# A retention layer with a token-mixing layer: tables and masks moved between engines, one pair form exchanged for another, the order planned anew

## The chip, the cores and the metric

The kernel runs on one core of a Trainium2 chip. The core has five engines that run side by side, each with its own instruction stream in a fixed order: TensorE (PE, matrix products), VectorE (DVE), ScalarE (ACT), GpSimd (POOL) and SyncE (SP, which here only issues transfers). Waits between them are semaphores set in when the program is built. SBUF is the working memory of 128 partitions; PSUM has eight banks of 128 x 512 float32, which PE writes and DVE and ACT read. The metric is the time of one execution in device microseconds. The kernel before was timed three times: 152.68, 157.84 and 153.59 us, median 153.59.

## The reference

Inputs q, k and v are float32 of shape (4, 8, 768, 64): batch, heads, tokens, width. Each head has a decay gamma = 1 - 2^(-5-h).

```
state = gamma * state + k[t] (outer) v[t]
y[t]  = (q[t] @ state) / 8
x     = y with the heads side by side           # (4, 768, 512)
W     = (x @ w_q) (x @ w_k)^T / 8               # tokens x tokens
out   = relu(W @ x) @ w_out                     # (4, 768, 512)
```

## The kernel before, in words

**Pairs.** The 768 tokens of a batch are three pairs of two chunks of 128 tokens, so there are twelve pairs over four batches (pair p is pair p % 3 of batch p // 3). Within a chunk the recurrence is computed as masked scores times v; between chunks a 64 x 64 state per head is carried in PSUM bank 7. The decay is applied as factors: v is multiplied by gamma^-t when it is cast to bfloat16, and the result by gamma^t.

**Kinds.** The string KINDS gives each pair a form. Form "2" (two tokens to a partition) keeps k and v as they are loaded, with two neighbouring tokens in one partition; its scores (L523), states, and products (L620, L631, L650) are made of more and smaller matmuls. Form "R" loads in the same way, but the casts (ck, cv) copy each 64-partition half into a one-token layout, four instructions instead of two, and then uses fewer matmuls (L537, L610, L664). Form "M" is R for k; its v is loaded already in the one-token layout, by four transfers of 256-byte rows (L177), and cast by two instructions of 128 partitions (L373) with the factor table fvM. Before, KINDS is 2R2RRR2RRMMM.

**Steps.** For each pair: loads Lk, Lq, Lv into one of 27 slots of the tile `stage`; casts ck, cq, cv; transposes trk, trq on PE into PSUM and their copies ek, eq (tiles kT, qT); scores sc by halves, and eat (L555), which multiplies them by the mask; st adds to the state and es copies it; in and ia form the product with the state and with the masked scores; ex (L685) multiplies by the factors fy into x; xt and exT transpose x. The mixing layer follows: wqk with its copy ew (tile m), zm per batch with its copy ez, mx and relu r (L798, L800), pj (L805) with w_out, eo copies the result to a slot, and S stores it.

**Order.** ORDER is a list of steps written out by a planner; the loop at the end of the kernel emits them one by one. A token such as `sc.7.0@05` is a step, its pair, its half and its PSUM banks; `:A`, `:V` and `:P` give the engine (ACT, DVE, POOL); `=4` gives a slot; `fill` is a matmul on a zero tile. Each engine executes its steps in this order. The framework adds a wait wherever a step touches what an earlier step of another engine still uses, slots, buffers and banks included. A step on two banks takes them as one strided slice:

```python
def two32(b):
    b0, b1 = b[:2]
    return banks[:, b0 : b1 + 1 : b1 - b0]
```

**Tables and masks.** The function `mask` makes a mask on POOL by a memset and an affine_select, twice where the partitions 64 to 127 have another offset, and copies the half over (L272 to L283). It is called by the tokens consts.2 and consts.R of ORDER, which stand among the first casts. The token constv.M, at about a third of ORDER, makes the table fvM: two iotas, a copy and a product on POOL (L230, L304, L305), then an Exp on ACT (L306). The tables fv and fy are made ahead of ORDER by DVE and ACT (L242 to L261).

The transfers are issued in the order of the L tokens on SP's queue, but for the first load, whose two halves go out on the queues of ACT and SP (FIRST).

Of the kernel before, what the change touches and what calls it, by code (L numbers as in the profile page):

```python
# [32 lines left out]
ck.7.1:P trq.5@45a xt.3@45b st.4.1 r.2.0:A r.2.1:A in.4.1@23 in.4.0@23 mx.0@01 exT.3:V cq.7.0:P  # L33
eq.5:A r.0.0:A ek.5:V ia.4.1@23 ia.4.0@23 wqk.3@4 r.0.1:A es.4.1:A sc.5.1@56 sc.5.0@01 cv.7.0:P
cv.7.1:P cv.8.1:P ex.4:V cv.8.0:P st.5.0 eat.5.0:V WO.0:A xt.4@2 pj.2.1@3 eat.5.1:V eo.2.1:A=12
pj.2.0@0 cv.9.0:P es.5.0:A ia.5.0@13 exT.4:V in.5.0@13 in.5.1@13 mx.1@56 r.1.0:V ia.5.1@13 ex.5:V
ew.3:V eo.2.0:A=12 pj.0.0@0 pj.0.1@2 ck.8.0:A xt.5@13a exT.5:V r.1.1:A eo.0.0:A=13 cq.6.1:A
trk.8@13b trk.6@04a trq.6@04b wqk.4@5 eq.6:A cq.8.0:A ek.8:V ek.6:V wqk.5@6 st.6.0 sc.6.0@04
cq.8.1:A ew.5:A ew.4:V sc.6.1@15 ck.10.1:P zm.1.0@3 ck.7.0:A eo.0.1:V=13 zm.1.1@3 cv.9.1:P eat.6.0:V
eat.6.1:V ez.1:A cq.7.1:A pj.1.1@6 cq.10.0:P cq.10.1:P cq.11.0:P cq.11.1:P trk.7@04a trq.8@04b  # L40
ck.11.0:P ck.11.1:P ek.7:V eo.1.1:A=15 mx.3@23 trq.7@15a pj.1.0@6 r.3.1:A r.3.0:A es.6.0:A eq.8:V
eq.7:V sc.8.1@04 cv.10.1:P cv.10.0:P mx.5@23 st.6.1 eo.1.0:A=15 r.5.1:A cq.9.1:A eat.8.1:V cq.9.0:A
r.5.0:A es.6.1:A ia.6.1@16 ia.6.0@16 in.6.1@16 ex.6:V sc.7.0@05 pj.3.1@4 st.7.0 sc.8.0@16 sc.7.1@23
eat.7.0:V eo.3.1:A=16 es.7.0:A pj.5.1@4 ck.9.0:A ck.9.1:A in.7.0@05 in.7.1@05 st.7.1 eat.7.1:V
ia.7.1@05 eat.8.0:V ia.7.0@05 trq.9@2 pj.3.0@3 ex.7:V xt.6@16a trk.9@16b eo.5.1:A=17 eq.9:A es.7.1:A
mx.4@05 r.4.0:A eo.3.0:V=16 st.8.0 r.4.1:A pj.5.0@2 ia.8.0@34 S.3 es.8.0:A ek.9:V exT.6:V
eo.5.0:A=17 sc.9.0@05 cv.11.0:P in.8.1@34 in.8.0@34 sc.9.1@16 st.9.0 S.5 es.9.0:A ck.10.0:A
eat.9.0:V ia.8.1@34 cv.11.1:P wqk.6@2 xt.7@0 pj.4.0@5 ew.6:A ex.8:V eat.9.1:V trk.10@2 st.9.1
trq.10@34a xt.8@34b in.9.1@16 eo.4.0:V=14 exT.7:A ek.10:A eq.10:V ia.9.0@16 ia.9.1@16 ex.9:V
pj.4.1@2 sc.10.1@05 exT.8:A eo.4.1:A=14 trq.11@34b sc.10.0@16 trk.11@34a wqk.8@2 eat.10.1:V ek.11:V  # L50
es.9.1:A eq.11:A S.0 ew.8:A wqk.7@0 eat.10.0:V ew.7:A sc.11.0@34 sc.11.1@25 st.10.0 zm.2.0@0
zm.2.1@0 es.10.0:A eat.11.1:V ez.2:A eat.11.0:V st.10.1 xt.9@1 es.10.1:A exT.9:A ia.10.1@25
ia.10.0@25 st.11.0 mx.6@06 es.11.0:A r.6.0:V r.6.1:A in.10.1@25 in.10.0@25 wqk.9@1 ia.11.0@34
ia.11.1@34 mx.7@06 in.11.1@34 in.11.0@34 ex.10:V pj.6.0@2 pj.6.1@5 r.7.0:A r.7.1:V ex.11:V mx.8@06
xt.10@34a xt.11@34b eo.6.0:A=19 eo.6.1:A=19 ew.9:V exT.11:V pj.7.1@1 wqk.11@5 exT.10:A wqk.10@3
r.8.1:A ew.10:A pj.8.1@4 ew.11:A r.8.0:A eo.7.1:V=20 zm.3.0@3 eo.8.1:V=18 zm.3.1@3 pj.7.0@0 ez.3:A
# [18 lines left out]
def kernel(  # L75
# [17 lines left out]

    nc = tc.nc
# [6 lines left out]
    U = 2  # L101
# [58 lines left out]
    def load(name, p, slot, part=None, eng=None):  # L160
# [7 lines left out]
        if KINDS[p] == "N" and name != "q":  # L168
# [60 lines left out]
    def iota(t, pattern, base, step, dtype=FP32):  # L229
# [5 lines left out]
    row = const_pool.tile([128, 3], mybir.dt.int32, name="row")  # L235
    tok = const_pool.tile([128, 1], FP32, name="tok")
# [5 lines left out]
    nc.vector.tensor_scalar(  # L242
        out=row[:, 1:2], in0=row[:, 0:1], scalar1=1, scalar2=U * (TG - 1), op0=ALU.logical_shift_left,
        op1=ALU.bitwise_and,
    )
    nc.vector.tensor_single_scalar(row[:, 2:3], row[:, 0:1], 6, op=ALU.logical_shift_right)
    nc.vector.tensor_tensor(out=tok, in0=row[:, 1:2], in1=row[:, 2:3], op=ALU.add)
# [5 lines left out]
    fy = const_pool.tile([128, NP * 2, H], FP32, name="fy")  # L253
    nc.vector.scalar_tensor_tensor(out=ty, in0=ty, scalar=tok, in1=ln_h, op0=ALU.add, op1=ALU.mult)
    nc.scalar.activation(out=fy, in_=ty, func=ACT.Exp)
# [6 lines left out]

    identity = const_pool.tile([128, 128], BF16, name="identity")
    make_identity(nc, identity)

    def mask(name, nj, step, base2):
        t = const_pool.tile([128, nj, U, TG], BF16, name=name)
        parts = [(t, 0)]
        if base2 is not None:
            parts.append((const_pool.tile([128, nj, U, TG], BF16, name=name + "_b"), base2))  # L270
        for a, base in parts:
            nc.gpsimd.memset(a, 1.0)  # L272
            nc.gpsimd.affine_select(
                out=a,
                in_=a,
                compare_op=ALU.is_ge,
                fill=0.0,
                base=base,
                pattern=[[-1, nj], [1, U], [U, TG]],
                channel_multiplier=-step,  # L280
            )
        if base2 is not None:
            nc.gpsimd.tensor_copy(out=t[64:128], in_=parts[1][0][64:128])  # L283
        return t.rearrange("p j u t -> p j (u t)")

    masks = {}
    fvs = {}

    def consts(kind):
        if kind == "2":  # L290
            masks["2"] = mask("mask2", 2, 2, 128)
        elif kind == "N":
            masks["N"] = mask("maskN", 1, 1, None)
        else:
            masks["R"] = mask("maskR", 1, 2, 127)

    def consts_v(kind):
        t = const_pool.tile([128, NP * 2, H], FP32, name="tv" + kind)
        f = const_pool.tile([128, NP * 2, H], FP32, name="fv" + kind)
        iota(t, [[C, NP * 2], [0, H]], 0, 1 if kind == "N" else 2)  # L300
        if kind == "M":
            t2 = const_pool.tile([128, NP * 2, H], FP32, name="tv2" + kind)
            iota(t2, [[C, NP * 2], [0, H]], 1 - C, 2)
            nc.gpsimd.tensor_copy(out=t[64:128], in_=t2[64:128])  # L304
        nc.gpsimd.tensor_tensor(out=t, in0=t, in1=ln_n, op=ALU.mult)  # L305
        nc.scalar.activation(out=f, in_=t, func=ACT.Exp)  # L306
        fvs[kind] = f
# [81 lines left out]
    def cq(e, b, p, x):  # L389
        st = pairs[p]  # L390
        if "qs" not in st:
# [491 lines left out]
```

## Time and profile before

| | |
|---|---|
| runs | 152.68, 157.84, 153.59 us; median 153.59 |
| profiled execution | 154.91 us, of which the span is 153.2 |
| mean granted TensorE clock | 0.833 |
| PE busy / DVE / ACT / POOL | 102.7 / 72.9 / 65.4 / 60.6 us |
| read from and written to memory | 20.19 and 6.29 MB |

The span goes from the first to the last instruction of the profiled execution. In the timelines a row is: start, duration, engine, line, operation, output and input, count, and in brackets the idle time of that engine before it with what ended it. The loads fill about the first 70 us; the stores come in the last third. The granted clock is a share of TensorE's full speed.

### The profile page before, as it was taken

To read this page: it belongs to the slowest core of one execution; us is meant where nothing else is said; L and a number is where in the kernel's file an instruction comes from. 1 tells how busy PE (TensorE), PEld (TensorE's weight loads), DVE (VectorE), ACT (ScalarE), POOL (GpSimd) and SP (SyncE) were. 2 spreads that over 40 slices of the span, in tenths; PEclk is the share of its full clock that TensorE was granted. 3 is DMA by queue.
4 is the path that set the end of the run, shared out by engine and by line. 5 is a ranking of instruction groups with operands and counts; after the bars stand their busy time and mean duration, and the time that the engine had idled before them with its cause. 6 is when DMAs were issued, how large, how long until landed. Compare 5 with 4: busy or idle time off the path is not lost.

```text
span 153.2 us, 3907 instructions
## 1 busy us (share of the span) xinstructions
PE 102.7 (67%) x1667; PEld 70.4 (46%) x1684; DVE 72.9 (48%) x117; ACT 65.4 (43%) x116; POOL 60.6 (40%) x89
## 2 busy tenths in 40 slices
PE   6958875599720997865365674569573766495990
PEld 2345554588520763743342443257452655263440
DVE  4045994567760376483533413143725733433460
ACT  4154256619404737537510705244244160435541
POOL 7599779879396699999100000000000000000000
PEclk9986999659985589999857655556999699999999
DMA  3999999999999999984000000342000000076394
GB/s 96 346 347 347 343 279 287 336 315 288 273 282 300 322 296 283 287 187 95 4 0 0 4 0 0 137 166 112 0 4 0 0 0 4 0 295 255 147 351 191
DMA packets 47169, 26.73 MB, mean 174 GB/s; under 512 B 8240, under 2 KB 44080, under 8 KB 47152
## 3 DMA queue, kind: packets, MB, share of 16 engines
q1 hardware_dynamic: 46624, 26.22, 56.1%
q10 hardware_dynamic: 528, 0.26, 0.6%
q8 instruction: 13, 0.21, 0.5%
q14 instruction: 4, 0.03, 0.1%
HBM read 20.19 MB, written 6.29 MB: 173 GB/s over the span
## 4 chain that ended last, share of the span: by engine, by line
PE 37%; SPq 21%; DVE 17%; ACT 9%; DMA 5%; issue 5%; POOL 4%; DVEq 0%; ACTq 0%; POOLq 0%
SPq L182 17%; PE banks L805 12%; DVE at L555 6%; DMA stage<-in_k_dram 5%; DVE x L685 5%; ACT relu L798 5%; PE banks L537 3%; SPq L199 3%; PE banks L664 3%; PE banks L727 2%; PE banks L738 2%; ACT qT L145 2%; PE banks L764 2%; DVE kT L146 2%; PE banks L694 2%
## 5 line engine op out<-in xcount | busy, mean ns | idle before, releaser
L805 PE MATMUL banks<-wout_sb,relu 128*128 128x512 bf16 x84 | 23.9, 406 | 9.5 <-DVE x L685 3.5
L555 DVE TENSOR_TENSOR at<-banks,maskR 128x1024 bf16<-128x1024 f32 x18 | 21.6, 1220 | 18.0 <-PE banks L537 7.6
L382 POOL TENSOR_TENSOR vs<-stage,fv 64x512 bf16<-64x512 f32 x24 | 25.0, 1043 | 2.9 <-DMA stage<-in_v_dram 1.5
L685 DVE TENSOR_TENSOR x<-banks,fy 128x1024 bf16<-128x1024 f32 x12 | 14.7, 1221 | 17.8 <-PE banks L664 7.7
L145 ACT COPY stage<-banks 128x512 f32<-128x512 f32 x15 | 8.7, 588 | 23.5 <-DVE at L555 6.9
L805 PEld LDWEIGHTS <-relu 128*128 128x128 bf16 x96 | 9.1, 103 | 18.4 <-issue 10.5
L145 ACT CAST ks<-stage 64x512 bf16<-64x512 f32 (+1 forms) x23 | 14.1, 616 | 6.6 <-DMA stage<-in_k_dram 6.3
L798 ACT ACTIVATE relu<-banks 128x512 bf16<-128x512 f32 x19 | 10.8, 597 | 11.8 <-PE banks L805 6.2
L146 POOL CAST ks<-stage 64x512 bf16<-64x512 f32 (+1 forms) x18 | 11.0, 609 | 5.7 <-DMA stage<-in_k_dram 5.0
L537 PE MATMUL banks<-qT,kT 64*128 64x128 bf16 x144 | 9.0, 263 | 5.7 <-DVE at L555 2.3
L328 PE MATMUL banks<-warm 128*128 128x512 bf16 x23 | 9.6, 575 | 1.8 <-DVE warm L218 1.3
L146 DVE COPY stage<-banks 128x512 f32<-128x512 f32 x9 | 6.1, 688 | 9.5 <-ACT relu L798 7.0
L537 PEld LDWEIGHTS <-kT 64*128 64x128 bf16 x144 | 6.0, 115 | 7.9 <-issue 6.6
L610 PE MATMUL banks<-s,qT 64*128 64x64 bf16 x128 | 4.2, 206 | 8.0 <-ACT relu L798 7.7
L664 PE MATMUL banks<-vs,at 128*128 128x64 bf16 x144 | 7.8, 209 | 2.6 <-DVE at L555 2.5
L727 PE MATMUL banks<-xT,wqk_w 128*128 128x256 bf16 x48 | 8.6, 309 | 1.4 <-DVE at L555 1.4
L145 ACT CAST qs<-stage 128x512 bf16<-128x512 f32 x13 | 7.7, 619 | 3.8 <-DMA stage<-in_q_dram 3.8
L555 DVE TENSOR_TENSOR at<-banks,mask 128x1024 bf16<-128x1024 f32 x6 | 7.2, 1222 | 3.6 <-ACT wqk_w L145 1.6
L571 PE MATMUL banks<-vs,ks 128*64 128x64 bf16 (+1 forms) x200 | 8.0, 217 | 1.3 <-POOL vs L363 0.9
L738 PE MATMUL banks<-wqk_w,xT 128*128 128x64 bf16 x96 | 8.7, 268 | 0.0
L664 PEld LDWEIGHTS <-at 128*128 128x128 bf16 x144 | 6.5, 108 | 4.5 <-issue 3.5
L146 DVE COPY kT<-banks 128x1024 bf16<-128x1024 bf16 x8 | 5.4, 685 | 5.9 <-PE banks L664 3.1
(89 smaller groups left out, 165.5 us busy)
## 6 DMA issues: line engine op xcount, KB each, us to landing
stage<-in_k_dram SPq DMA_DIRECT2D x12, 512.0 KB, 6.4
stage<-in_q_dram SPq DMA_DIRECT2D x11, 512.0 KB, 7.0
stage<-in_v_dram SPq DMA_DIRECT2D x9, 512.0 KB, 6.9
out_dram<-stage SPq DMA_DIRECT2D x9, 512.0 KB, 2.9
stage<-in_v_dram SPq DMA_DIRECT2D x12, 128.0 KB, 3.8
out_dram<-stage SPq DMA_DIRECT2D x6, 256.0 KB, 2.0
stage<-in_moe_w_out_dram SPq DMA_DIRECT2D x4, 256.0 KB, 4.5
stage<-in_q_dram ACTq DMA_DIRECT2D x1, 256.0 KB, 4.1
```

The lines of the kernel that those rows point to most:

```text
L145: return nc.scalar.copy(out=out, in_=in_)
L146: return ENGINES[e].tensor_copy(out=out, in_=in_)
L182: eng.dma_start(out=st.rearrange("g (h f) -> g h f", h=H)[:, hs], in_=src.rearrange("h (g j) d -> g h (j d)", j=2)[:, hs],)
L382: eng.tensor_tensor(out=st["vs"][rows(j), c].rearrange("p hp x d -> p (hp x) d"), in0=src[rows(c), :, j], in1=fv[rows(c), cp, :, j].to_bro ...
L537: nc.tensor.matmul(out=at[:, x, hi, c], lhsT=kT[rows(x), hp, c], rhs=qT[rows(x), c, hp], start=(hi == 0 and c == 0), stop=(hi == 1 and c = ...
L555: ENGINES[e].tensor_tensor(out=st["at", half].rearrange("p x hi j t -> p x (hi j t)").rearrange("p x (n f) -> p x n f", n=n), in0=st["at_p ...
L664: nc.tensor.matmul(out=y[:, x, c, hp, :], lhsT=at[:, x, hi, c, :], rhs=vr[:, c, hp, x, :], start=first(p, x), stop=False, skip_group_check ...
L685: ENGINES[e].tensor_tensor(out=dst, in0=src, in1=f.to_broadcast([128, 2, H, D]), op=ALU.mult)
L727: nc.tensor.matmul(out=ps[:, 128:384], lhsT=wqk_sb[:, a, 0 : 2 * DH], rhs=st["xT"][:, a].rearrange("p c t -> p (c t)"), start=(a == 0), st ...
L738: nc.tensor.matmul(out=wk[:, c], lhsT=st["xT"][:, a, c, :], rhs=wqk_sb[:, a, 2 * DH :], start=False, stop=(a == NDM - 1), skip_group_check ...
L798: nc.scalar.activation(out=st["relu", c], in_=src, func=ACT.Relu)
L805: nc.tensor.matmul(out=bank32(b[0]), lhsT=st["relu", c][:, a // 2, a % 2, :], rhs=wout_sb[:, a, :], start=(a == 0), stop=(a == NDM - 1),)
```

## The change

Tables: the argument of the Exp for the M pairs (now fvm) is formed by DVE from a per-partition token number, and its Exp stands in ACT's prologue beside the other two. Masks: an iota `tf` holds the token number of each column, and DVE compares it with the token number of the partition, once per mask plane. The tokens consts and constv are gone. KINDS becomes RR2RRRRRMMMM: pairs 0 and 6 go from form 2 to R, pair 8 from R to M, and pair 2 alone keeps form 2. FIRST is now k of pair 0. ORDER is a new list: other engines for some steps, other banks, other places for the fills (35 matmuls instead of 28) and the loads. Code for a layout with U = 8 is added and not used, since U is 2; trq is written in a more general way and does the same.

```diff
-KINDS = "2R2RRR2RRMMM"
-FIRST = ('q', 0, 0)
+KINDS = "RR2RRRRRMMMM"
+FIRST = ('k', 0, 0)
...
-    nc.vector.scalar_tensor_tensor(out=ty, in0=ty, scalar=tok, in1=ln_h, op0=ALU.add, op1=ALU.mult)
-    nc.scalar.activation(out=fy, in_=ty, func=ACT.Exp)
+    def decay(name, tok, ln):
+        t = const_pool.tile([128, NP * 2, H], FP32, name="t" + name)
+        f = const_pool.tile([128, NP * 2, H], FP32, name=name)
+        nc.vector.scalar_tensor_tensor(out=t, in0=ty, scalar=tok, in1=ln, op0=ALU.add, op1=ALU.mult)
+        nc.scalar.activation(out=f, in_=t, func=ACT.Exp)
+        return f
+
+    fy = decay("fy", tok_q, ln_h)
...
+        fvs["M"] = decay("fvm", tok_r, ln_n)
...
-    def mask(name, nj, step, base2):
...
-            nc.gpsimd.memset(a, 1.0)
-            nc.gpsimd.affine_select(
...
-            nc.gpsimd.tensor_copy(out=t[64:128], in_=parts[1][0][64:128])
+    def mask(name, toks):
+        t = const_pool.tile([128, len(toks), C], BF16, name=name)
+        for j, tok in enumerate(toks):
+            nc.vector.tensor_scalar(out=t[:, j], in0=tf, scalar1=tok, scalar2=None, op0=ALU.is_ge)
+        return t
...
-    def consts_v(kind):
...
-        nc.gpsimd.tensor_tensor(out=t, in0=t, in1=ln_n, op=ALU.mult)
-        nc.scalar.activation(out=f, in_=t, func=ACT.Exp)
```

A part of ORDER from the second third, of before and of after (pairs 3 to 5):

```diff
-sc.3.0@45 es.3.0:A wqk.0@6 xt.2@2 wqk.1@3 exT.2:V eat.3.0:V trk.4@0 ew.0:A cq.4.1:A cq.4.0:A st.3.1
-fill.1@1 ia.3.1@26 wqk.2@1 ek.4:A trq.4@45a ck.6.0:P ck.8.1:P es.3.1:V ew.1:V cq.6.0:P in.3.1@26
-ia.3.0@26 ck.5.0:A ck.6.1:P ew.2:V eq.4:V cv.6.0:P zm.0.0@3 zm.0.1@3 cv.6.1:P sc.4.1@45 sc.4.0@01
-ez.0:A st.4.0 cq.5.1:A ex.3:V eat.4.1:V eat.4.0:V mx.2@23 es.4.0:A cq.5.0:A trk.5@6 constv.M
+st.3.0 xt.2@1 ck.4.1:A ew.0:A trk.4@05a trq.4@4 eat.3.1:V es.3.0:V eq.4:V cq.8.1:P cq.8.0:P cv.6.1:P
+cq.7.0:P cq.7.1:P sc.3.0@26 exT.2:A ek.4:A eat.3.0:V wqk.2@1 st.3.1 sc.4.1@05 in.3.1@34 ia.3.0@34
+eat.4.1:V ia.3.1@34 wqk.1@2 ck.5.1:A ew.2:A ck.7.1:P es.3.1:A cq.5.1:A ew.1:A trk.5@1 cq.5.0:A
+sc.4.0@05 cv.7.0:P ex.3:V st.4.0 zm.0.0@2 zm.0.1@2 ez.0:A es.4.0:A xt.3@3 eat.4.0:V cv.7.1:P
```

More of the change, by code (lines that the diff above doesn't have):

```diff
@@ L167, in load @@
         hs = slice(0, H) if part is None else slice(part, H, 2)
-        if KINDS[p] == "N" and name != "q":
+        if name == "q" and U == 8:
+            f = slice(0, 2) if part is None else part
+            eng.dma_start(
+                out=st.rearrange("p (x f) -> p x f", x=2)[:, f],
+                in_=src.rearrange("h (t u) d -> t h (u d)", u=U)[:, hs],
+            )
+        elif KINDS[p] == "N" and name != "q":
             for c in cs:
@@ L241, with shifted, token @@
     iota(ty, [[C, NP * 2], [0, H]], 0, 0)
[L242 to L247, printed above, removed]
+    tf = const_pool.tile([128, C], FP32, name="tf")
+    iota(tf.rearrange("p (u t) -> p u t", u=U), [[1, U], [U, TG]], 0, 0)
+    def shifted(i, shift, mask):
+        op = ALU.logical_shift_left if shift >= 0 else ALU.logical_shift_right
+        nc.vector.tensor_scalar(
+            out=row[:, i : i + 1], in0=row[:, 0:1], scalar1=abs(shift), scalar2=mask, op0=op,
+            op1=ALU.bitwise_and,
+        )
+    def token(name, a, b):
+        t = const_pool.tile([128, 1], FP32, name=name)
+        if isinstance(b, int):
+            nc.vector.tensor_single_scalar(t, row[:, a : a + 1], b, op=ALU.add)
+        else:
+            nc.vector.tensor_tensor(out=t, in0=row[:, a : a + 1], in1=row[:, b[0] : b[0] + 1], op=ALU.add)
+        return t
+    shifted(1, 1, C - 2)
+    shifted(2, -6, 1)
+    tok_r = token("tok_r", 1, [2])
+    if U == 2:
+        tok_q = tok_r
+    else:
+        shifted(3, 3, 8 * (TG - 1))
+        shifted(4, -4, U - 1)
+        tok_q = token("tok_q", 3, [4])
     fv = const_pool.tile([128, NP, H, 2], FP32, name="fv")
@@ L250 @@
     nc.scalar.activation(out=fv, in_=tv, func=ACT.Exp)
-    fy = const_pool.tile([128, NP * 2, H], FP32, name="fy")
-    nc.vector.scalar_tensor_tensor(out=ty, in0=ty, scalar=tok, in1=ln_h, op0=ALU.add, op1=ALU.mult)
-    nc.scalar.activation(out=fy, in_=ty, func=ACT.Exp)
+    def decay(name, tok, ln):
[5 more added lines that the diff above has]
+    fy = decay("fy", tok_q, ln_h)
+    fvs = {}
+    if "M" in KINDS:
+        fvs["M"] = decay("fvm", tok_r, ln_n)
+    if "N" in KINDS:
+        tok_n = token("tok_n", 0, 0)
+        fvs["N"] = decay("fvn", tok_n, ln_n)
+    identity = const_pool.tile([128, 128], BF16, name="identity")
+    make_identity(nc, identity)
+    if U > 2:
+        ident_q = const_pool.tile([128, 128], BF16, name="ident_q")
+        nc.vector.tensor_copy(
+            out=ident_q.rearrange("p (c hp t) -> p c t hp", c=2, hp=HP),
+            in_=identity.rearrange("p (c t hp) -> p c t hp", c=2, hp=HP),
+        )
+    def mask(name, toks):
+        t = const_pool.tile([128, len(toks), C], BF16, name=name)
+        for j, tok in enumerate(toks):
+            nc.vector.tensor_scalar(out=t[:, j], in0=tf, scalar1=tok, scalar2=None, op0=ALU.is_ge)
+        return t
+    masks = {}
+    if "2" in KINDS:
+        masks["2"] = mask("mask2", [token(f"tok_2{j}", 1, j) for j in range(2)])
+    if "N" in KINDS:
+        masks["N"] = mask("maskN", [tok_n])
+    if any(kind in KINDS for kind in "RMH"):
+        masks["R"] = mask("maskR", [tok_r])
     fy1 = const_pool.tile([128, NP * 2, 2, HP], FP32, name="fy1")
@@ L832 @@
             b = ["ab".index(i) if i in "ab" else int(i) for i in b]
-        if name in ("consts", "constv"):
-            (consts if name == "consts" else consts_v)(args[0])
-            continue
         args = [int(i) for i in args]
```

150 lines of the change are left out of this document (58 added, 92 removed).

## The prediction

> **What bounds the kernel now.** I read the page's engine sums first, then the chain that ended last, then the stretches of ten microseconds, then each engine's own timeline around the places where PE stands still.
>
> ```profile
> span 153.2 us, 3907 instructions
> PE 102.7 (67%) x1667; PEld 70.4 (46%) x1684; DVE 72.9 (48%) x117; ACT 65.4 (43%) x116; POOL 60.6 (40%) x89
> PE 37%; SPq 21%; DVE 17%; ACT 9%; DMA 5%; issue 5%; POOL 4%; DVEq 0%; ACTq 0%; POOLq 0%
> ```
>
> No engine is full. The chain is loads at first (SPq 21%) and then a hand-over between PE, DVE and ACT. Where it leaves the loads is a place of its own, seen in the chain in order of time and in the timelines of ACT and PE:
>
> ```profile
> 34.15 7.73 DMA stage<-in_k_dram
> 45.21 2.01 POOL vs L363 x2
> 47.91 0.30 POOL tvM L305
> 48.37 1.07 ACT relu L798 x2
> ```
>
> ```profile
> 48.22 0.24 ACT L306 ACTIVATE fvM<-tvM 128x48 f32<-128x48 f32 x1 [7.00 <-POOL tvM L305]
> 49.49 0.61 PE L610 MATMUL banks<-s,qT 64*128 64x64 bf16 x16 [6.26 <-ACT relu L798]
> ```
>
> ACT comes to the Exp that makes the table fvM (step constv.M) and waits 7.00 us, since POOL forms its argument only behind k casts whose load lands at 41.9 and the products of v behind them. The two relus stand behind that Exp, and PE stands still for 6.26 us. After 49.5 the chain holds no load any more, so what is won here is won at the end unless something else takes it.
>
> ```profile
> 10.00:20.00 10.00, 8.59 (x195) 5.72 (x197) 7.30 (x10) 4.29 (x8) 8.11 (x12) 0.83 1.14 342
> 30.00:40.00 10.00, 9.84 (x188) 8.46 (x183) 6.32 (x10) 4.60 (x9) 8.51 (x9) 0.77 1.04 306
> 90.00:100.00 10.00, 5.73 (x59) 2.88 (x60) 3.01 (x4) 3.14 (x6) 0.00 (x0) 0.50 0.14 52
> 110.00:120.00 10.00, 4.88 (x101) 3.83 (x102) 4.91 (x5) 3.79 (x7) 0.00 (x0) 0.99 0.01 2
> ```
>
> Columns: PE, PEld, DVE, ACT and POOL busy, granted clock, DMA share, GB/s. Early, PE is busy 8.6 to 9.8 of 10 us; late, about 5, with DVE and ACT as idle as PE. The reason stands in PE's timeline together with the two bank numbers behind each step's @ in ORDER:
>
> ```profile
> 26.31 0.41 PE L523 MATMUL banks<-qT,kT 64*64 64x128 bf16 x14 [1.34 <-ACT xT L145]
> 76.27 1.04 PE L650 MATMUL banks<-vs,at 64*128 64x64 bf16 x32 [1.62 <-DVE at L555]
> 77.81 0.29 PE L537 MATMUL banks<-qT,kT 64*128 64x128 bf16 x1
> 79.26 0.58 PE L537 MATMUL banks<-qT,kT 64*128 64x128 bf16 x7 [1.17 <-DVE x L685]
> 88.39 0.53 PE L664 MATMUL banks<-vs,at 128*128 128x64 bf16 x7 [1.26 <-DVE at L555]
> 140.27 0.84 PE L764 MATMUL banks<-x,m 128*64 128x256 bf16 x12 [0.74 <-ACT relu L798]
> ```
>
> The step at 77.81 is sc.7.0@05: its first matmul writes bank 0 and runs, its second writes bank 5 and waits 1.17 us for ex.6, which reads banks 1 and 6 and nothing of bank 5. A pair of banks is addressed as one strided range (banks[:, b0:b1+1:b1-b0]), and the built program holds a wait for everything that lies between the two ends. I call this a **range wait**: the two steps share neither a bank nor a value. In the built program of before I count 18 on PE, 3 of them in the first half of ORDER. All 18 show in the timeline as idle time, the first 1.34 and the last 0.74 above, 21.0 us together, 1.17 each. DVE and ACT have 45 more, on PE and on each other. The early, full stretches are those where ORDER uses neighbouring pairs (01, 23, 45), which have nothing between them.
>
> **The change, part by part.**
>
> *Table and masks.* The Exp for the M pairs moves into ACT's prologue, with its argument from DVE, so the 7.00 us wait cannot come back in that form. What is late next at 43 us? ACT's relus have their inputs; the loads run ahead (last POOL product below). I count the PE idle, **-6.3 us**. The added DVE work ahead of the casts is two token sums, one 128x48 product and three 128x128 comparisons.
>
> ```profile
> 8.00 0.55 DVE L146 CAST ks<-stage 128x512 bf16<-128x512 f32 x1 [4.67 <-DMA stage<-in_k_dram]
> 4.94 0.62 ACT L145 CAST qs<-stage 128x512 bf16<-128x512 f32 x1 [1.97 <-DMA stage<-in_q_dram]
> ```
>
> The comparisons have no row. Even at the 0.55 us of the 128x512 cast each, with the small ones under 0.3, they come to about 2.5 us beside DVE's 4.67 us wait for the first k; ACT's further 0.23 us Exp fits into its 1.97. Cost 0; without that cover 2.5. The mask work that leaves POOL was off the chain: 0. The first pair changes more: ACT alone casts q (2 x 0.62) and k (now 4 x 0.62), where DVE took half of k, and k now loads first. This puts the first scores up to 1 us later, before pair 1's data allow the next step: 0, up to +1.
>
> *Pairs 0 and 6 from two-token to one-token form.* The full pair has 120 matmuls in the old form and 64 in the new, in scores, state, inter and intra steps.
>
> ```profile
> 65.21 0.88 PE L523 MATMUL banks<-qT,kT 64*64 64x128 bf16 x32 [0.18 <-DVE kT L146]
> 39.42 0.62 PE L537 MATMUL banks<-qT,kT 64*128 64x128 bf16 x16
> 109.96 0.64 PE L664 MATMUL banks<-vs,at 128*128 128x64 bf16 x16
> ```
>
> Scores fall from 0.88 to 0.62 and intra from 1.04 (the 76.27 row) to 0.64, so 0.66 per pair, 1.3 for two; the state and inter steps can give as much again. Between 0 (PE waits anyhow) and -2.6 I take **-1.0**, near PE's 37% of the chain. The extra cast instructions (two for k and two for v per pair) fall to ACT and POOL.
>
> *Pair 8's v in 256-byte rows.* Both kinds are issued by SP; the columns after the count are shortest, median and longest issue in ns.
>
> ```profile
> L177 SPq DMA_DIRECT2D stage<-in_v_dram x12: 633/685/1456, 52.3 to 68.4; - x12
> L182 SPq DMA_DIRECT2D stage<-in_v_dram x9: 492/1461/2859, 1.3 to 49.1; - x9
> 69.45 4.04 POOL L373 TENSOR_TENSOR vs<-stage,fvM 128x512 bf16<-128x512 f32 x4
> 88.73 1.04 PE L488 MATMUL banks<-identity,qs 128*128 128x128 bf16 x8
> ```
>
> Four issues of 685 ns replace one of 1461: +1.3 us of SP's queue, for pair 8 and all loads behind it. On POOL two products of 1.04 us replace four, which returns 2.1. The cover: POOL's last product ends at 73.5, while PE first touches pair 9 at 88.7. Cost 0; without that cover +1.3.
>
> *Engine shares.* Counting steps by engine, times the means of their rows, POOL loses about 6 us, ACT gains about 7 (ten more k casts, five more m casts, six relus fewer) and DVE is level. ACT would be at 72 of 153 us: 0 by itself.
>
> *The new order.* It is the part that decides. In the built program of after, PE has **33 range waits against 18**, 15 of them in the first half of ORDER against 3; over all engines 115 against 63. Of the 102 PE steps on a pair of banks, 9 use neighbours, against 56. So the order of after has, from its second pair on, what before has only from its middle. The price of one more wait: from below 0, where PE or DVE would have waited for its own data; from above the 1.17 of the 18 rows. A stretch of the new order can be walked: eat.3.1, es.3.0, eq.4, ek.4, eat.3.0, sc.4.1, in.3.1, ia.3.0, eat.4.1.
>
> ```profile
> L555 DVE TENSOR_TENSOR at<-banks,maskR 128x1024 bf16<-128x1024 f32 x18 | 21.6, 1220 | 18.0 <-PE banks L537 7.6 <-PE banks L738 3.2 <-ACT xT L145 2.4
> L145 ACT COPY kT<-banks 128x1024 bf16<-128x1024 bf16 x4 | 4.0, 1012 | 4.2 <-PE banks L449 2.2 <-PE banks L700 1.2 <-PE banks L433 0.7
> L146 DVE COPY qT<-banks 128x1024 bf16<-128x1024 bf16 x7 | 4.7, 684 | 3.7 <-ACT relu L798 1.6 <-PE banks L488 1.2 <-PE banks L700 0.9
> L146 DVE CAST s<-banks 128x256 bf16<-128x256 f32 x6 | 2.5, 418 | 2.6 <-PE banks L571 2.6
> ```
>
> ```profile
> 17.98 0.40 PE L537 MATMUL banks<-qT,kT 64*128 64x128 bf16 x8
> 18.62 0.29 PE L610 MATMUL banks<-s,qT 64*128 64x64 bf16 x8 [0.24 <-DVE s L146]
> 18.84 0.41 PE L664 MATMUL banks<-vs,at 128*128 128x64 bf16 x8
> ```
>
> With its range waits each of these stands behind the one before: three products of 1.22, 0.42, 0.68, 1.01 and the PE steps 0.40 + 0.29 + 0.41 make 6.9 us. DVE's own five make 4.8. Three range waits in a row (eat.3.0 on ek.4, sc.4.1 on eat.3.0, eat.4.1 on ia.3.0) thus cost 2.1, or 0.7 each. Between 0.7 and 1.17 I take 0.8, near the walk because the added waits lie mostly early, as it does: 15 x 0.8 = **+12.0 us**, with 0 and 17.6 as ends. The added range waits of DVE and ACT are taken as part of this price.
>
> **Sum.** 153.2 - 6.3 - 1.0 + 12.0 = 157.9 us of span. The profiled execution took 154.91, 1.7 beyond its span, and lies 1.3 above the median 153.59; on the median's scale this is 157.9 + 1.7 - 1.3 = **158.3 us**, 3.1% slower. About 2% (150.5 to 156.7) is what a measurement of this kernel can tell from no change.
>
> **The rivals.**
>
> *The added waits cost little (faster).* One mechanism: the new order puts a range wait mostly where PE would wait for that engine's next result anyhow. For: DVE and ACT have idle time in each stretch. Against: all 18 of before show as idle. At price 0 it gives 153.2 - 7.3 = 145.9, 146.3 on the median's scale. Break-even is 7.3 / 15 = 0.49 per wait, and faster by 2% needs less than 0.28. Chance 0.20.
>
> *The middle (within 2%).* Prices from 0.28 to 0.69 give 150.5 to 156.7: the stall's gain is handed back by the waits. Chance 0.23.
>
> *The clock holds.* Rows of shorter stretches:
>
> ```profile
> 30.00:34.00 4.00, 4.00 (x70) 3.33 (x65) 2.48 (x3) 0.37 (x1) 3.31 (x4) 0.50 1.08 321
> 50.00:54.00 4.00, 4.00 (x52) 3.02 (x46) 1.23 (x1) 2.63 (x5) 2.89 (x4) 0.50 1.09 321
> 80.00:100.00 20.00, 12.13 (x138) 7.04 (x140) 6.59 (x7) 6.35 (x12) 0.00 (x0) 0.59 0.07 27
> ```
>
> PE ran at half clock behind the 6.26 us gap, and in 30 to 34 and most of 80 to 100 too. If only long gaps lowered the clock, an order with gaps near 1 us would run at 1.0 throughout and save half of 4.00, half of 4.00 and 0.41 x 12.13, 9.0 us together: 149.3 us. Against it stand the longest idle times of PE ahead of 30 and in 80 to 100:
>
> ```profile
> 28.11 0.37 PE L620 MATMUL banks<-s,qT 64*128 64x64 bf16 x4 [1.39 <-DVE at L555]
> 84.66 1.02 PE L805 MATMUL banks<-wout_sb,relu 128*128 128x512 bf16 x4 [1.94 <-ACT stage L145]
> ```
>
> 1.39 and 1.94 us were enough there. Chance 0.06. The Trainium skill ("TensorE: Matmul & The Clock Gate", "HAM oscillation — how this bites in real kernels") states this rule with a limit of about 3.4 us of idle time; the two stretches speak against it here.
>
> *A new stall of the old kind (slower still).* A cast on ACT or POOL queued ahead of needed work waits for its load, as the 7.00 us did; at half to all of that, 162 to 165. New places for it are the two w_out casts on POOL and the later k casts on ACT. Chance 0.08, inside slower.
>
> *The change doesn't do what it says:* excluded for the table, since in after's program all three Exps stand ahead of ACT's first cast.
>
> **How the numbers follow.** Forecast 0.43 (own range 156.7 to 163); new stall or prices over 1.1 0.08; middle 0.23; cheap waits 0.20; clock 0.06. So slower 0.51, same 0.23, faster 0.26. The range from 147 to 167 takes in most of the cheap-wait case down to near price 0 and the ends 17.6 and the new stall; it leaves out under 2 in 10.
>
> **What would show it.** Right: no ACT wait of 7 us and no PE idle over 3 us near 43; PE waits of about 1 us on DVE and ACT already between 20 and 50 us; a PE share under 8 of 10 there; loads over by 73 and off the chain. The prediction is wrong if PE's stretches from 20 to 50 us are as full as before's (then the price is near 0), or if a load ends a wait on the chain after 50 us.

## The result

The changed kernel took 173.73 us (median of 172.13 to 174.46) where the kernel before, run beside it, took 154.25. The ratio is 1.129, with a 95% interval from 1.115 to 1.143: clearly slower, by four times the 3.1% that was forecast and beyond the upper end of the range, 167. Its profiled execution took 173.88 us with a span of 172.1. Some executions of a kernel come out a few per cent longer, at a lower granted clock: the ratios here and below leave these out, the medians take in all.

The page of the changed kernel, span, engine sums and chain:

```profile
span 172.1 us, 3717 instructions
PE 114.9 (67%) x1574; PEld 75.1 (44%) x1587; DVE 75.3 (44%) x122; ACT 73.5 (43%) x127; POOL 56.1 (33%) x72
PE 52%; DVE 24%; ACT 14%; issue 5%; DMA 3%; SPq 0%; DVEq 0%; ACTq 0%
```

Two things stand here. The loads have left the chain (SPq from 21% to 0), as forecast. And PE is *busier* by 12.2 us (102.7 before) with 93 matmul records fewer. The work has not grown; its pieces take longer. The rest of the span, in which PE is idle, went from 50.5 to 57.2 us, although the 6.3 us stall is gone. Three numbers are needed below: 12.2 us more busy, 6.7 more idle, 18.9 in all.

The stretch from 20 to 50 us, before and then in the changed kernel (columns as in the prediction: PE, PEld, DVE, ACT, POOL busy, granted clock, DMA share, GB/s):

```profile
20.00:50.00 30.00, 18.36 (x422) 15.41 (x423) 17.77 (x22) 14.51 (x26) 24.14 (x32) 0.80 1.02 295
20.00:50.00 30.00, 19.37 (x315) 15.61 (x312) 13.80 (x16) 14.01 (x23) 25.11 (x30) 0.58 1.05 304
```

The changed kernel's PE is two thirds busy, at 0.58 of full clock, and gets through 315 matmuls where before did 422 with its 6.3 us stall inside. So the sign that was to show the prediction wrong, stretches as full as before's, came true by the letter (19.37 us busy against 18.36), and yet the price is far from near 0: a busy share counts slow work as busy. PE's longest waits in the whole execution, from the view that sums waits by line (total, times, longest):

```profile
PE banks L683 <- DVE at L574: 4.0, 4, 1.4
PE banks L824 <- DVE relu L819: 3.9, 3, 2.0
PE banks L802 <- ACT xT L145: 2.4, 1, 2.4
PE banks L517 <- DVE x L704: 1.8, 1, 1.8
```

No single wait is large; the longest is 2.4 us. The stretch that the prediction walked, eat.3.1 to eat.4.1, as it ran. DVE's timeline, then PE's:

```profile
41.03 1.23 DVE L574 TENSOR_TENSOR at<-banks,maskR 128x1024 bf16<-128x1024 f32 x1 [1.68 <-PE banks L513]
42.17 0.41 DVE L146 CAST s<-banks 128x256 bf16<-128x256 f32 x1
42.50 0.68 DVE L146 COPY qT<-banks 128x1024 bf16<-128x1024 bf16 x1
44.32 1.23 DVE L574 TENSOR_TENSOR at<-banks,maskR 128x1024 bf16<-128x1024 f32 x1 [1.13 <-ACT kT L145]
47.89 1.23 DVE L574 TENSOR_TENSOR at<-banks,maskR 128x1024 bf16<-128x1024 f32 x1 [2.35 <-PE banks L683]
```

```profile
46.49 0.61 PE L556 MATMUL banks<-qT,kT 64*128 64x128 bf16 x8
46.89 0.42 PE L629 MATMUL banks<-s,qT 64*128 64x64 bf16 x8
47.24 0.61 PE L683 MATMUL banks<-vs,at 128*128 128x64 bf16 x8
49.17 0.58 PE L683 MATMUL banks<-vs,at 128*128 128x64 bf16 x8 [1.32 <-DVE at L574]
```

The hand-overs are there: eat.3.0 (44.32) behind ek.4 on ACT, eat.4.1 (47.89) behind ia.3.0, and sc.4.1 (46.49) behind eat.3.0, which ends at 45.55. The walk gave 6.9 us; from 41.03 to 49.12 it took 8.1. Part of the difference is wqk.2, which the walk left out: it waits for ek.4 too (a range wait again) and, with st.3.1 behind it, keeps PE from sc.4.1 for 0.9 us beyond 45.55. The other part is that the three PE steps (0.61, 0.42 and 0.61, overlapping) took 1.36 us from 46.49 to 47.85 where the walk had 0.40 + 0.29 + 0.41 = 1.10.

When x of pairs 3 and 6 is written (DVE, tile x), before and after:

```profile
39.94 1.23 DVE L685 TENSOR_TENSOR x<-banks,fy 128x1024 bf16<-128x1024 f32 x1 [0.82 <-ACT z L145]
77.98 1.23 DVE L685 TENSOR_TENSOR x<-banks,fy 128x1024 bf16<-128x1024 f32 x1 [1.77 <-PE banks L631]
```

```profile
49.79 1.22 DVE L704 TENSOR_TENSOR x<-banks,fy 128x1024 bf16<-128x1024 f32 x1 [0.68 <-PE banks L683]
89.16 1.23 DVE L704 TENSOR_TENSOR x<-banks,fy 128x1024 bf16<-128x1024 f32 x1 [4.37 <-PE banks L477]
```

x of pair 3 is 9.9 us late already, at a point of the work that before reaches ahead of its stall; x of pair 6 is 11.2 us late although that stall is behind it. The other parts of the change, in the changed kernel's timelines (the table's Exp, a plane of a mask, the last v issues of SP, the last product of POOL):

```profile
2.82 0.23 ACT L285 ACTIVATE fvm<-tfvm 128x48 f32<-128x48 f32 x1
2.85 0.28 DVE L309 TENSOR_SCALAR mask<-tf,tok 128x128 bf16<-128x128 f32 x1
60.68 7.31 SPq L183 DMA_DIRECT2D stage<-in_v_dram  x8
70.91 1.04 POOL L390 TENSOR_TENSOR vs<-stage,fvm 128x512 bf16<-128x512 f32 x1 [0.52 <-DMA stage<-in_v_dram]
```

### The profile page after: what moved, and what is told of

Its sections match the earlier page's. It is cut to its first block, busy times and chain, and to the rows that moved or that the text cites. A ratio compares the mean times of both kernels' runs of the same rounds, so it can differ in the third digit from the quotient of the medians.

```text
span 172.1 us, 3717 instructions
## 1 busy us (share of the span) xinstructions
PE 114.9 (67%) x1574; PEld 75.1 (44%) x1587; DVE 75.3 (44%) x122; ACT 73.5 (43%) x127; POOL 56.1 (33%) x72
## 4 chain that ended last, share of the span: by engine, by line
PE 52%; DVE 24%; ACT 14%; issue 5%; DMA 3%; SPq 0%; DVEq 0%; ACTq 0%
PE banks L824 15%; DVE at L574 12%; DVE x L704 6%; PE banks L746 5%; PE banks L683 5%; PE banks L757 4%; PE banks L556 4%; ACT xT L145 3%; DMA stage<-in_q_dram 3%; ACT relu L817 3%; PE banks L629 2%; ACT ks L145 2%; PE banks L719 2%; DVE relu L819 2%; PE banks L783 2%
## 5 line engine op out<-in xcount | busy, mean ns | idle before, releaser
L574 DVE TENSOR_TENSOR at<-banks,maskR 128x1024 bf16<-128x1024 f32 x22 | 26.7, 1223 | 31.5 <-PE banks L683 5.3
L824 PE MATMUL banks<-wout_sb,relu 128*128 128x512 bf16 x84 | 29.4, 474 | 7.8 <-DVE relu L819 3.9
L399 POOL TENSOR_TENSOR vs<-stage,fv 64x512 bf16<-64x512 f32 x26 | 27.9, 1072 | 9.6 <-DMA stage<-in_v_dram 8.0
L145 ACT CAST ks<-stage 64x512 bf16<-64x512 f32 (+1 forms) x33 | 20.3, 616 | 0.5
L145 ACT CAST m<-banks 128x384 bf16<-128x384 f32 x12 | 5.7, 481 | 18.4 <-DVE at L574 8.8
L817 ACT ACTIVATE relu<-banks 128x512 bf16<-128x512 f32 x13 | 7.5, 597 | 11.9 <-DVE x L704 3.6
L145 ACT COPY qT<-banks 128x1024 bf16<-128x1024 bf16 x7 | 7.1, 1012 | 10.6 <-PE banks L513 4.2
L145 ACT COPY xT<-banks 128x1024 bf16<-128x1024 bf16 x6 | 6.1, 1012 | 12.4 <-DVE at L574 4.5
L819 DVE TENSOR_SCALAR relu<-banks 128x512 bf16<-128x512 f32 x11 | 7.1, 686 | 8.5 <-ACT relu L817 6.1
L757 PEld LDWEIGHTS <-xT 128*128 128x128 bf16 x96 | 9.4, 154 | 1.1
```

What stands on the lines that cost most here:

```text
L145: return nc.scalar.copy(out=out, in_=in_)
L399: eng.tensor_tensor(out=st["vs"][rows(j), c].rearrange("p hp x d -> p (hp x) d"), in0=src[rows(c), :, j], in1=fv[rows(c), cp, :, j].to_bro ...
L574: ENGINES[e].tensor_tensor(out=st["at", half].rearrange("p x hi j t -> p x (hi j t)").rearrange("p x (n f) -> p x n f", n=n), in0=st["at_p ...
L757: nc.tensor.matmul(out=wk[:, c], lhsT=st["xT"][:, a, c, :], rhs=wqk_sb[:, a, 2 * DH :], start=False, stop=(a == NDM - 1), skip_group_check ...
L817: nc.scalar.activation(out=st["relu", c], in_=src, func=ACT.Relu)
L819: nc.vector.tensor_relu(out=st["relu", c], in_=src)
```

## The experiments

Four questions: is it the range waits or something else in the order; what is each other part of the change worth; how much of a range wait's price is the granted clock; and does a version beat both kernels. Theory **R** says that range waits are what the change costs. Its rival **O** says that it is the order itself: which engine does what, and which step needs whose value.

### Banks renamed

One permutation of the numbers 0 to 6 is applied to every bank in ORDER. Steps, engines, order on each engine, values and tiles stay, and so does which steps share a bank. What changes is only what lies *between* the two ends of a pair. For the changed kernel with few range waits:

```diff
-cq.7.0:P cq.7.1:P sc.3.0@26 exT.2:A ek.4:A eat.3.0:V wqk.2@1 st.3.1 sc.4.1@05 in.3.1@34 ia.3.0@34
+cq.7.0:P cq.7.1:P sc.3.0@45 exT.2:A ek.4:A eat.3.0:V wqk.2@0 st.3.1 sc.4.1@12 in.3.1@36 ia.3.0@36
```

The three others are made in the same way; two tokens from each (changed kernel with many, kernel before with few and with many):

```diff
-sc.4.1@05 in.3.1@34
+sc.4.1@04 in.3.1@26
...
-ia.6.1@16 ... sc.7.0@05
+ia.6.1@01 ... sc.7.0@23
...
-ia.6.1@16 ... sc.7.0@05
+ia.6.1@03 ... sc.7.0@46
```

> The changed kernel with the PSUM banks 0 to 6 renamed (to 2, 0, 4, 3, 6, 1, 5) in every entry of the written order: same instructions, same order on every engine, same values; only the banks that lie between the two ends of a pair change. TensorE's range waits fall from 33 to 14 (those in the first half of the order from 15 to 7), those of all engines from 115 to 53. Theory R (the added range waits are what the change costs, at the price that the result gives them, 1.79 us for each added one of TensorE or 0.52 us for each added one of any engine): 173.7 - 19 x 1.79 = 140 us by the one, 173.7 - 62 x 0.52 = 141.6 us by the other; 138 to 150 us. Theory O (the new order itself, that is which engine does what and which step waits for which value, and range waits cost nothing): 171 to 175 us, no change from the changed kernel.

> The changed kernel with the banks renamed the other way (to 4, 5, 3, 2, 6, 0, 1): TensorE's range waits rise from 33 to 39, those of all engines from 115 to 130. Theory R: 173.7 + 6 x 1.79 = 184 us, or 173.7 + 15 x 0.52 = 181.5 us. Theory O: 172 to 175 us.

> The kernel before, its order untouched, with the banks renamed (to 4, 0, 2, 5, 1, 6, 3) so that TensorE's range waits rise from 18 to 40 (from 3 to 17 in the first half) and those of all engines from 63 to 119, about what the changed kernel has. Theory R: 154.3 + 56 x 0.52 = 183 us, or 154.3 + 22 x 1.79 = 194 us; at the price of the prediction, 0.8, 172 us. Less by what the 6.3 us wait on the loads hides of it: 170 to 194 us. Theory O: 153 to 156 us.

> The kernel before with the banks renamed (to 2, 1, 6, 5, 4, 3, 0) so that TensorE's range waits fall from 18 to 12 and those of all engines from 63 to 34. Theory R: 154.3 - 6 x 1.79 = 143.5 us, or 154.3 - 29 x 0.52 = 139 us; at 0.8 each 149.5 us; 138 to 150 us. Theory O: 153 to 156 us.

Measured (range waits counted in the built programs; span, busy and clock of the profiled execution; idle is the span less PE's busy time; the row of before has the median of its runs beside these four, and the profile shown ahead of the prediction):

| kernel | range waits PE / all | median us | ratio to before [95%] | span | PE busy | PE idle | clock |
|---|---|---|---|---|---|---|---|
| changed, few | 14 / 53 | 125.2 | 0.810 [0.798, 0.823] | 124.3 | 94.5 | 29.8 | 0.93 |
| changed | 33 / 115 | 173.7 | 1.129 [1.115, 1.143] | 172.1 | 114.9 | 57.2 | 0.76 |
| changed, many | 39 / 130 | 182.5 | 1.169 [1.151, 1.188] | 178.5 | 115.0 | 63.5 | 0.78 |
| before, few | 12 / 34 | 132.7 | 0.846 [0.833, 0.860] | 128.6 | 97.0 | 31.6 | 0.91 |
| before | 18 / 63 | 155.1 | 1 | 153.2 | 102.7 | 50.5 | 0.83 |
| before, many | 40 / 119 | 183.7 | 1.188 [1.167, 1.209] | 181.6 | 116.2 | 65.4 | 0.76 |

O is out as the account of what the change costs: renaming seven banks, with not one instruction moved, takes 48 us from the changed kernel and adds 29 to the one before. R holds in sign and order everywhere, and its size was still too low for the two kernels with few (140 expected, 125.2 came; 139 to 143.5 expected, 132.7 came). The same instructions in the changed kernel with few range waits, the page and DVE's timeline (the same five steps as above, and x of pair 6):

```profile
span 124.3 us, 3733 instructions
PE 94.5 (76%) x1587; PEld 61.5 (49%) x1587; DVE 74.3 (60%) x122; ACT 72.7 (58%) x127; POOL 56.0 (45%) x72
```

```profile
32.28 1.23 DVE L574 TENSOR_TENSOR at<-banks,maskR 128x1024 bf16<-128x1024 f32 x1 [0.86 <-PE banks L556]
33.42 0.41 DVE L146 CAST s<-banks 128x256 bf16<-128x256 f32 x1
33.90 0.69 DVE L146 COPY qT<-banks 128x1024 bf16<-128x1024 bf16 x1
34.50 2.57 DVE L574 TENSOR_TENSOR at<-banks,maskR 128x1024 bf16<-128x1024 f32 x2
...
59.28 1.22 DVE L704 TENSOR_TENSOR x<-banks,fy 128x1024 bf16<-128x1024 f32 x1 [0.59 <-PE banks L783]
```

```profile
20.00:50.00 30.00, 23.32 (x499) 18.37 (x499) 21.66 (x24) 23.02 (x41) 25.93 (x30) 0.94 1.06 306
```

The five steps now run back to back, 32.28 to 37.07: 4.8 us, DVE's own time as the prediction had it, against 8.1. The range waits of this stretch cost 3.3 us, the slower PE steps between them included, not the 2.1 of the walk. In 20 to 50 us PE runs 499 matmuls instead of 315, at 0.94. A step on two banks costs DVE the same 1.2 us whether the banks are neighbours or not, so it is not the distance that is slow to access, but the wait.

The price of a PE range wait differs widely: from the changed kernel 48.5 / 19 = 2.6 us to its few and 8.8 / 6 = 1.5 to its many, from the kernel before 22.4 / 6 = 3.7 to its few and 28.6 / 22 = 1.3 to its many. Per range wait of any engine it is 0.78, 0.58, 0.77 and 0.51. So the count over all engines gives the steadier price, and of the kernel before with many it had said 183 us where PE's count said 194. Neither gives one price, and no run separates the waits of one engine from those of another, since they rise together.

### The parts of the change, in the old order

The early table alone, in the kernel before:

```diff
-ez.0:A st.4.0 cq.5.1:A ex.3:V eat.4.1:V eat.4.0:V mx.2@23 es.4.0:A cq.5.0:A trk.5@6 constv.M
+ez.0:A st.4.0 cq.5.1:A ex.3:V eat.4.1:V eat.4.0:V mx.2@23 es.4.0:A cq.5.0:A trk.5@6 ck.7.1:P
...
+    consts_v("M")
     for token in ORDER:
```

> The kernel before with one edit: the M pairs' table is made ahead of the loop over the order (the token constv.M goes, the same function is called just before the loop), so its Exp no longer waits behind k casts on POOL. Range waits as before, 18 on TensorE and 63 on all engines. Theory T (the prediction's first term, the 6.3 us that TensorE stood still are won at the end): about 148 us where the kernel before takes 154 to 155. Rival: the stall is worth nothing, since the range waits behind it take it back, 153 to 156 us. In between, 150 to 152 us: about half of it is won.

Measured: 147.28 us against 156.07, ratio 0.966 [0.949, 0.983], so 5.2 us by the ratio (2.6 to 7.9). Theory T holds. In its timelines the Exp stands in the prologue, and the PE step that had stood still 6.26 us (in.4.1, L610) follows without a wait:

```profile
3.13 0.24 ACT L306 ACTIVATE fvM<-tvM 128x48 f32<-128x48 f32 x1
```

```profile
40.62 0.32 PE L571 MATMUL banks<-vs,ks 128*64 128x64 bf16 x8
40.87 0.41 PE L610 MATMUL banks<-s,qT 64*128 64x64 bf16 x16
```

All of the change but the order and the first load, then the same with the pair kinds of before, so that only tables and masks differ from before:

```diff
-fill.15@6 Lq.0=1 Lv.0=2 cv.0.1:V cq.0.0:A cq.0.1:A ck.0.1:A Lk.1=3 ck.0.0:A Lq.1=4 fill.5@0 trq.0@0
+fill.15@6 Lv.0=1 cq.0.1:P cv.0.1:P Lk.0=2 cq.0.0:A Lq.1=3 ck.0.1:A ck.0.0:V Lk.1=4 Lv.1=5 Lk.2=6
...
 KINDS = "RR2RRRRRMMMM"
-FIRST = ('k', 0, 0)
+FIRST = ('q', 0, 0)
```

```diff
-KINDS = "RR2RRRRRMMMM"
+KINDS = "2R2RRR2RRMMM"
```

> The changed kernel's tables, masks, pair kinds and 256-byte rows with the written order of the kernel before (its constants' tokens left out, the first pair's loads as before): all of the change but the new order. Range waits 18 on TensorE and 63 on all engines, as before. By the prediction's terms without its +12.0: 154.5 - 6.3 - 1.0 = 147 us; 145 to 150 us. If the parts other than the order are worth nothing: 153 to 156 us. If they themselves cost what was lost: 165 us or more.

> The kernel with the changed tables and masks and the order of before, now with the pair kinds of before too (2R2RRR2RRMMM): it differs from the kernel before only in how tables and masks are made. It tells which part of the change held the kernel with the old order at 150.5 us where the early table alone gave 147.3. If the new pair kinds cost about 3 us in the old order: 146 to 148.5 us. If it is the masks and tables made ahead of the casts: 149.5 to 152 us.

Measured: 150.52 us, ratio 0.984 [0.972, 0.996], just above the 145 to 150 expected, and with the old pair kinds 146.63, ratio 0.961 [0.942, 0.980]. So tables and masks give about 6.0 us (0.039 x 154), which can't be told from the early table alone, and the new pair kinds cost 2.3%, 3.5 us, where the prediction had a gain of 1.0; the two intervals just overlap. The range waits are 18 and 63 in both kernels. Where the pair kinds lose, in DVE's and POOL's timelines, with the old kinds first and the new ones second (k's first casts, POOL's products of v beside them, x of pair 0):

```profile
6.60 2.05 POOL L380 TENSOR_TENSOR vs<-stage,fv 128x512 bf16<-128x512 f32 x2 [1.41 <-DMA stage<-in_v_dram]
7.98 0.95 DVE L146 CAST ks<-stage 128x512 bf16<-128x512 f32 x1 [4.42 <-DMA stage<-in_k_dram]
...
17.92 1.22 DVE L704 TENSOR_TENSOR x<-banks,fy 128x1024 bf16<-128x1024 f32 x1
```

```profile
6.29 4.52 POOL L399 TENSOR_TENSOR vs<-stage,fv 64x512 bf16<-64x512 f32 x4 [1.41 <-DMA stage<-in_v_dram]
7.73 2.18 DVE L146 CAST ks<-stage 64x512 bf16<-64x512 f32 x2 [4.17 <-DMA stage<-in_k_dram]
...
19.95 1.21 DVE L704 TENSOR_TENSOR x<-banks,fy 128x1024 bf16<-128x1024 f32 x1
```

Pair 0 is the first work, so its two extra casts have nothing to hide behind. DVE's share of k takes 2.18 us instead of 0.95, and pair 0 ends 2.0 us later. That delay is still 1.9 us at x of pair 6; how the rest of the 3.5 us comes about was not followed.

Both together, with the banks renamed as in the kernel before with few (12 range waits on PE, 34 in all):

```diff
-r.5.0:A es.6.1:A ia.6.1@16 ia.6.0@16 in.6.1@16 ex.6:V sc.7.0@05 pj.3.1@4 st.7.0 sc.8.0@16 sc.7.1@23
+r.5.0:A es.6.1:A ia.6.1@01 ia.6.0@01 in.6.1@01 ex.6:V sc.7.0@23 pj.3.1@4 st.7.0 sc.8.0@01 sc.7.1@56
```

> The kernel of all of the change but the order, with its banks renamed (to 2, 1, 6, 5, 4, 3, 0): 12 range waits on TensorE, 34 on all engines. The kernel before took 132.7 us with that renaming alone. Sum of both, if they add up: 132.7 - 7.3 = 125.4 us; if the first wait on the loads is what bounds the renamed kernel (its TensorE was busy 3.55 of 10 us in the stretch from 40 to 50 us), more is won: 122 to 125 us. If the new order is itself better than the old one at equal range waits, this stays behind the renamed changed kernel's 125.2 us: 128 to 133 us.

Measured: 126.49 us, ratio 0.820 [0.796, 0.845]. The two gains add up (125.4 expected). The old order with 12 PE range waits and the new one with 14 are level, 126.5 and 125.2 us, their intervals overlapping. So with most range waits gone on both sides, the new order is no worse than the old: what the order costs, it costs by its range waits.

### The clock

Five matmuls of zeros, into unused columns of bank 7, ahead of each PE step that has a range wait; the waits stay:

```diff
+    def keep(n):
+        for _ in range(n):
+            nc.tensor.matmul(
+                out=banks[:, 7, 256:512], lhsT=warm[:, 0:128], rhs=warm[:, 0:256], start=False, stop=False,
+                skip_group_check=True,
+            )
...
-eat.3.0:V wqk.2@1 st.3.1 sc.4.1@05 in.3.1@34 ia.3.0@34 eat.4.1:V ia.3.1@34
+eat.3.0:V keep.5 wqk.2@1 st.3.1 keep.5 sc.4.1@05 in.3.1@34 ia.3.0@34 eat.4.1:V keep.5 ia.3.1@34
```

> The changed kernel with five matmuls of zeros (256 columns each) into unused columns of bank 7 put ahead of each of its 33 TensorE steps that have a range wait; the waits, the order and the values stay. At full clock the five take about 1.1 us (a 512-column fill matmul took 0.43), less than most of the idle times they fill, so they are no work in themselves but keep TensorE going. Theory C (a part of the cost of a range wait is the lower granted clock that follows the idle time): granted clock 0.76 up to 0.88 or more, 160 to 167 us. If the clock isn't set by these idle times, or PE's clock isn't what the hand-overs wait for: clock 0.74 to 0.80 and 173 to 185 us, since the added matmuls delay some steps.

Measured in the changed kernel: 156.87 us, 17 less than without, ratio to before 1.018 [0.994, 1.043]. More work, and a tenth faster. The page, the added matmuls and the stretch from 20 to 50 us:

```profile
span 155.9 us, 4047 instructions
PE 114.7 (74%) x1739; PEld 76.1 (49%) x1752; DVE 75.2 (48%) x122; ACT 73.5 (47%) x127; POOL 56.1 (36%) x72
```

```profile
L354 PE MATMUL banks<-warm 128*128 128x256 bf16 x165 | 24.8, 283 | 4.8 <-ACT s L148 3.8 <-DVE s L149 0.9
```

```profile
20.00:50.00 30.00, 21.75 (x408) 17.09 (x409) 15.89 (x17) 16.69 (x28) 25.30 (x29) 0.94 1.00 289
```

PE's own work takes 114.7 - 24.8 = 89.9 us instead of 114.9, and the clock goes from 0.76 to 0.97. So 25 us of the changed kernel's PE time were low clock. Theory C holds, beyond its 160 to 167 us, with the clock worth 17 of the changed kernel's 174 us. It may be worth more, since the added matmuls can cost something themselves (they waited 4.8 us for copies of the state in bank 7).

The same in the kernel before (18 steps), and in the renamed changed kernel (14 steps, with five and with three):

```diff
+        elif name == "keep":
+            keep(args[0])
```

> The kernel before, its order and banks untouched, with the five zero matmuls ahead of each of its 18 TensorE steps that have a range wait. In the changed kernel this raised the clock from 0.76 to 0.97, took TensorE's own busy time (without the added matmuls) from 114.9 to 89.9 us and gave 17 us, two thirds of these 25. Theory C: the kernel before, with 102.7 us busy at 0.83, comes to about 91 us of its own busy time at 0.95 or more, and gains two thirds of 12, 8 us: 145 to 150 us. If before's clock is lowered mainly by its one long idle time of 6.3 us, which has none of these steps ahead of it: 152 to 157 us.

> The renamed changed kernel (14 range waits on TensorE) with the five zero matmuls ahead of each of these 14 steps. TensorE was busy 94.5 us at a clock of 0.93; its low stretch was 75 to 90 us (0.52 in 80 to 90). Theory C: its own busy time falls to about 89 us, of which two thirds, 3 to 4 us, reach the end: 120 to 123 us. If the five matmuls delay more than the clock returns, since fewer of the idle times are as long as they are: 126 to 130 us.

> The same with three zero matmuls at each of the 14 steps, 0.65 to 0.85 us instead of 1.1 to 1.4. If the delay by the added matmuls counts, this is faster than with five by up to 14 x 0.4 = 5 us: 118 to 122 us. If the clock needs the longer filling: 123 to 126 us, no gain over the renamed kernel's 125.2.

Measured: the kernel before 152.02 us, ratio 0.967 [0.935, 0.998]; the clock rises from 0.83 to 0.90 in the profiled execution, 152.9 us of span. A gain, but its size is not settled by that interval, which holds both C's 145 to 150 us and the other theory's 152. The renamed changed kernel 126.50, ratio 0.813 [0.781, 0.845], with five, and 124.33, ratio 0.807 [0.795, 0.819], with three, against 0.810 [0.798, 0.823] without. No difference that can be told, although with three the clock goes from 0.93 to 0.98; the gain that C expected of five, 120 to 123 us, did not come. The page with three, and its added matmuls:

```profile
span 122.9 us, 3803 instructions
PE 94.6 (77%) x1615; PEld 62.7 (51%) x1629; DVE 74.1 (60%) x122; ACT 72.7 (59%) x127; POOL 56.1 (46%) x72
```

```profile
L352 PE MATMUL banks<-warm 128*128 128x256 bf16 x42 | 7.2, 283 | 5.3 <-ACT s L146 4.4 <-DVE s L147 0.9
```

PE's own work falls from 94.5 to 87.4 us, and the end moves by about 1. The added matmuls themselves waited 5.3 us for copies of the state. Whether such waits take the gain back, or PE's pace no longer sets the end where few range waits are left, no run tells. The renamed changed kernel and this variant of it beat the kernel before by 19% and the changed one by 28%.

## Why the prediction was wrong

**What bounds the kernel.** Right, and more so than written: the range waits that the prediction found in PE's timeline set the time of both kernels. The kernel before loses 22 us to those 29, of its 63, that one renaming removes.

**The stall, -6.3.** Right: 5.2 us (2.6 to 7.9) alone, 6.0 with the masks. The 7.00 us wait does not come back, no load stands on the chain after the first (it lands at 6.1), and the last one that POOL waits for is there at 70.9 (forecast: over by 73).

**Tables and masks, 0.** Right. A mask took 0.28 us, half of the bound of 0.55, beside DVE's wait for the first v.

**Pair kinds, -1.0, and the first pair, 0 to +1.** Wrong in sign in the old order: +3.5 us. The step counted PE's matmuls, which were not what was late, and put the extra casts on engines with room; the first pair has no room, and 2.0 us of delay start there. In the changed order this pair's casts are on other engines, and its share there was not measured: x of pair 0 starts at 20.66 us there, 1.05 later than before.

**256-byte rows, 0, and ACT's load, 0.** Nothing speaks against them: the loads are off the chain, and with ACT busy 72.7 us the renamed kernel still runs in 124.3.

**The added range waits, +12.0: the step that failed.** The mechanism was right, the term mis-sized. The order alone is the step from ratio 0.984 to 1.129, 22 us of 154 (that is 1.5 for each of the 15, not 0.8). Set against the profiled execution with the old order, whose page has

```profile
span 151.7 us, 3702 instructions
PE 103.9 (69%) x1563; PEld 70.6 (47%) x1580; DVE 75.6 (50%) x124; ACT 66.1 (44%) x117; POOL 60.8 (40%) x80
```

the changed kernel has 57.2 - 47.8 = 9.4 us more PE idle time, 0.63 per added PE range wait. (That execution lies 3 us above its kernel's median, so the split is rough.) The 0.7 of the walked stretch comes near this price of the *idle time*, in part by luck: as it ran, that stretch lost 3.3 us to its three waits, 1.1 each. What the price left out is the 11.0 us more *busy time*, 0.73 per wait: the gaps also lower the clock of the work behind them. The zero matmuls show that this is the clock and that it reaches the end: 17 us with all 33 waits in place. The upper end of 17.6 had the same gap, since 1.17 was idle time too. The step also took the 37 added range waits of DVE and ACT into PE's price without a sum of their own; the renamings speak for counting them, but their share was not measured.

The prediction had the evidence: it quoted half clock behind gaps of 1.39 and 1.94 us, and used it only to argue that the clock would not rise. The consequence for an order with fifteen more such gaps, that the clock would fall, was not drawn. The rival on the clock went the wrong way for the same reason: it asked only how much higher the clock might go. It also priced the clock from three stretches, at 9.0 us, where the page of before, 102.7 us busy at 0.833, holds about 17 (an estimate: 102.7 x 0.167), more than any term of the sum. The Trainium skill ("TensorE: Matmul & The Clock Gate", "HAM oscillation — how this bites in real kernels") gives a limit of about 3.4 us of idle time; the changed kernel's longest PE wait is 2.4 us, and its clock is 0.58 over 30 us, so the trace does not agree.

**The sum as it was measured.** About -6 for the tables, +3.5 for the pair kinds in the old order, +22 for the order: 19.5 us, against 19.5 between the medians. The three are steps of one chain of ratios, so that they add up proves nothing more. The prediction's -6.3 - 1.0 + 12.0 made 4.7.

## What to carry to other kernels

In these kernels a strided slice over two PSUM banks waits for everything between its ends, so the choice of bank numbers is part of the schedule: count such waits in the built program and rename banks before anything else. When a change adds short waits to TensorE, price each twice, once as idle time and once for the lower clock of the matmuls behind it; here, by a rough split, the second half was as large as the first (11.0 and 9.4 us). A gain found by removing one stall is only as safe as the waits of the order around it.

## What the runs showed of the hardware

- Eight gaps of 0.9 to 1.8 us within 30 us (20 to 50) went with a granted clock of 0.58; matmuls of zeros ahead of the waiting steps brought 0.94 in the same stretch, and 17 us at the end. With few range waits left, the step from 0.93 to 0.98 brought nothing that could be measured (124.3 us against 125.2).
- DVE's cast of 128 x 512 float32 took 0.55 us in the kernel before (the prediction's row at 8.00), where POOL stood between these two products:

```profile
6.55 1.04 POOL L363 TENSOR_TENSOR vs<-stage,fv 128x512 bf16<-128x512 f32 x1 [1.24 <-DMA stage<-in_v_dram]
9.12 1.05 POOL L363 TENSOR_TENSOR vs<-stage,fv 128x512 bf16<-128x512 f32 x1
```

  It took 0.95 us beside a POOL product, and casts of 64 x 512 beside POOL products took 1.09 each (the two traces under the pair kinds). The Trainium skill ("SBUF — State Buffer", "Terms") says that the two engines share a port pair, which one holds for its whole instruction while the other is blocked; the lengthening agrees in direction, and no run here tells a block from sharing.
